# V of two chunks loaded behind the key transpose, and the crossbar transposes of those chunks issued in thirds, in a fused attention and feed-forward kernel

## The chip, the cores and the metric

The kernel runs on one core of one Trainium2 chip. The metric is device time in microseconds (us) of one execution. Before the change it is 226.85 us, the median of 3 runs.

## The reference

Attention with two kinds of heads feeds a feed-forward block with a leaky ReLU.

```python
# q, k, v: (4 batches, 8 heads, 768 positions, 64); is_retrieval = [1,0,1,0,0,0,1,0]; n_sink 4, window 64
scores = (1.0 / np.sqrt(D)) * np.matmul(q, k.transpose(0, 1, 3, 2))
# heads 0, 2, 6 ("retrieval"): causal.  The others ("stream"): causal, and only the
# first 4 keys (the sink) and the last 64 keys up to the query
a = softmax(np.where(mask, scores, -1e9))
attn = np.matmul(a, v)
x = attn.transpose(0, 2, 1, 3).reshape(B * S, H * D)      # 3072 x 512
h = x @ w_in                                              # 512 x 2048
out = np.maximum(0.01 * h, h) @ w_out                     # 2048 x 512, float32
```

All inputs and the output are float32 in HBM. The kernel computes in bfloat16 with float32 accumulation.

## The kernel before, in words

The 3072 rows are cut into 8 chunks of 384 positions: 4 batches times 2 halves. Chunks are worked in the order (batch 0, half 0), (1, 0), (0, 1), (1, 1), (2, 0), (3, 0), (2, 1), (3, 1), numbered 0 to 7; the change concerns chunks 2 and 3, the second halves of batches 0 and 1. Within a chunk, the three tiles of 128 positions are the "thirds".

Every chunk goes through four stages. Loads: `load_qk` (L113) and `load_v` (L121) issue, on GpSimd's queue, three DMAs each for K, Q and V, one for each third; such a DMA also converts float32 to bfloat16. Transposes: attention wants the head dimension on the partitions. For chunks 2 to 7 `turn_dma` (L240) does that with two crossbar DMA transposes on SyncE's queue, kb to kd for keys and qb to qd for queries, 128 x 1536 elements each. VectorE then copies the transposed keys into `kt` (`spreads`, L247, copies at L253: six for each chunk, one for each third and half of the heads). Stream heads read V shifted by 64 positions as well: `v_shift` (L147) writes `vb` from `va` by two DMAs on SyncE's queue (L151, L152), which wait for V to land. Attention: `Attention` (L294) issues scores (L345, L380) on TensorE, exponentials on ScalarE, masks on VectorE, and the products with V (L314), which read `va` and `vb`, some slots later. Feed-forward: `in_slots` multiplies by w_in (L585), and `Pair` (L720) multiplies by w_out (L753) with a seven-product scheme whose sums of weights and activations (L714, L736) and corrections (L768) VectorE makes.

The order on every engine is written out by hand: the tile framework runs in manual schedule mode, so instructions stand on an engine's queue in the order of the program, and waits are semaphores. The part around the change, with its lines:

- L886 to L890: the last loads issued ahead of the compute: three quarters of w_out, K and Q of chunk 2 (L888), the last quarter of w_out, V of chunk 2 (L890).
- L1008 to L1011: transposes of chunk 2, the shift of its V, then the loads of K, Q and V of chunk 3.
- L1018 to L1020: transposes of chunk 3, then the loads of K, Q and V of chunk 4. The shift of V of chunk 3 comes at L1032.
- L1034 to L1037: attention of chunk 2 merged with the feed-forward products of chunks 0 and 1; then the key copies of chunk 3.

The buffers kb and qb have one slot each, so loading the K of one chunk waits until the transpose of the chunk before has read it.[...] For two later chunks the kernel already holds GpSimd's queue back by a 1x1 copy into a tile `hold` that reads a tile written by a transpose (L1085).

Of the kernel before, what the change touches and what calls it, by code (L numbers as in the profile page):

```python
# [21 lines left out]
def kernel(  # L22
# [12 lines left out]
    nc = tc.nc  # L35
# [26 lines left out]
    def bf(name, *shape):  # L62
        return one.tile([128, *shape], BF16, name=name)
# [17 lines left out]
    hold = bf("hold", 1)  # L81
# [17 lines left out]
    raw = {}  # L99
# [13 lines left out]
    def load_qk(n, nms="kq"):  # L113
        b, c = ORDER[n]
        for nm in nms:
            t = rot.tile([128, 3, H, D], BF16, name=f"{nm}b", tag=f"{nm}b", bufs=1)
            raw[nm, n] = t
            for g in range(3):
                nc.gpsimd.dma_start(out=t[:, g], in_=nat[nm][b, c, :, :, g])  # L119

    def load_v(n, gs=range(3)):  # L121
        b, c = ORDER[n]
        for g in gs:
            nc.gpsimd.dma_start(out=va[b][:, 3 * c + g, :, 0:D], in_=nat["v"][b, c, :, :, g])  # L124

# [17 lines left out]
    def load_out(i):  # L143
        c = slice(4 * i, 4 * i + 4)
        nc.gpsimd.dma_start(out=w_out_bf[:, c, :], in_=w_out_r[:, c, :])

    def v_shift(n, eng=None):  # L147
        eng = eng or nc.sync
        i, c = ORDER[n]
        lo, hi = (0, 2) if c == 0 else (2, 5)  # L150
        eng.dma_start(out=vb[i][0:64, lo:hi], in_=va[i][64:128, lo:hi, 1:H])  # L151
        eng.dma_start(out=vb[i][64:128, lo:hi], in_=va[i][0:64, lo + 1 : hi + 1, 1:H])  # L152
# [87 lines left out]
    def turn_dma(n):  # L240
        qx[n] = rot.tile([128, 3, 4, 128], BF16, name="qd", tag="qd", bufs=3)
        raw["kx", n] = rot.tile([128, 3, 4, 128], BF16, name="kd", tag="kd", bufs=2)
        for nm, dst in (("k", raw["kx", n]), ("q", qx[n])):
            nc.sync.dma_start_transpose(out=dst.rearrange("p g q t -> p (g q) t"),
                                        in_=raw[nm, n].rearrange("p g h d -> p (g h d)"))

    def spreads(n):  # L247
        b, c = ORDER[n]
# [362 lines left out]
    for i, t in ((1, va[1]), (3, vb[1])):  # L611
        t = t.rearrange("p g h d -> p (g h d)")[:, 0 : 2 * KH * 512].rearrange("p (x g c) -> p x g c", x=2, g=KH)
# [98 lines left out]
    def weight_sums(half):  # L711

        r = slice(NH // 2 * half, NH // 2 * half + NH // 2)
        sub = lambda o, x, y: nc.vector.tensor_tensor(o[:, r], x[:, r], y[:, r], op=ALU.subtract)  # L714
        sub(w1, T3, B11)
        sub(w2, B22, w1)
        sub(T3, B22, T3)
        sub(w4, B21, w2)
# [76 lines left out]
    def tiles_of(n):  # L795
        return [tt for tt in range(3) if tt != spare(n)]
# [5 lines left out]
    for n in range(NCH):  # L802
        t = tiles_of(n)
# [66 lines left out]
    nc.gpsimd.iota(diff[:], pattern=[[1, 128]], base=0, channel_multiplier=-1, allow_small_or_imprecise_dtypes=True)  # L870
    load_tile(1)
    load_v(0, (0,))
    load_sinks(0)
    load_sinks(1)
    load_v(0, (1,))
    load_tile(2)
    load_v(0, (2,))
    load_in(0, 512)
    load_qk(1, "k")
# [7 lines left out]
        load_out(i)  # L887
    load_qk(2)  # L888
    load_out(3)
    load_v(2)  # L890


    nc.vector.tensor_scalar(ident[:], diff[:], 0.0, None, op0=ALU.is_equal)
# [13 lines left out]
    for a in (ats4[0], ats[0]):  # L907
# [4 lines left out]
                         in_=blank[:, 0:128].rearrange("p (o f) -> p o f", o=1).to_broadcast([128, 4, 128]), func=ACTF.Copy)  # L912
    nc.scalar.activation(out=ats[1][:, :, 1:3, :].rearrange("p j e f -> p j (e f)"),
                         in_=blank[:, 0:128].rearrange("p (o f) -> p o f", o=1).to_broadcast([128, 3, 128]), func=ACTF.Copy)
# [91 lines left out]
    zero_keys(1, nc.vector, CH, S)  # L1006
    nc.vector.memset(va[2][:, :, :, D], 1.0)
    turn_dma(2)  # L1008
    v_shift(2)
    load_qk(3)  # L1010
    load_v(3)  # L1011
    weight_sums(0)
    for i in range(1, 5):
        pairs[0].sum(i)
# [1 line left out]
    run(p1[:14], steps(0, ("P1",)), p1[14:])  # L1016
    weight_sums(1)
    turn_dma(3)  # L1018
    load_qk(4)
    load_v(4)  # L1020
    run(steps(1, ("P1",)), steps(0, ("P6", "P2")))
# [17 lines left out]
    for n in range(2, NCH):  # L1039
        a, extra = [], ()  # L1040
        if n + 2 < NCH:
            turn_dma(n + 2)
            v_shift(n + 2)
            extra = spreads(n + 2)
            if ORDER[n + 2][1] == 0:
                load_sinks(ORDER[n + 2][0])
            if n + 3 < NCH:
                load_qk(n + 3, "k" if n > 2 else "kq")
                if n < 3:
                    load_v(n + 3)  # L1050
            if ORDER[n + 2][1] == 0:
                sink_values(ORDER[n + 2][0], nc.gpsimd)
# [73 lines left out]
```

## Time and profile before

| what | value |
|---|---|
| median of 3 runs (lowest to highest) | 226.85 us (226.79 to 227.56) |
| profiled execution | 227.62 us, span 225.8 us, granted clock 1.00 |
| TensorE, VectorE, ScalarE, GpSimd busy | 95%, 66%, 60%, 32% of the span |
| DMA queue of GpSimd (software) | 77552 packets, 13.37 MB |
| DMA queue of SyncE (hardware) | 34336 packets, 15.14 MB |
| V third, issue to landing (24 of them) | least 2.7, median 7.0, most 14.3 us |
| crossbar transpose of a chunk's keys, issue to landing (6) | least 5.1, median 6.9, most 9.5 us, where the trace has it |

The span is the time from the first to the last instruction in one profiled execution. A timeline row gives the start, the duration, the engine, the line, the operation and its operands, and in brackets how long the engine stood idle before it and what ended that. Matmuls overlap in the pipeline: a row's duration includes its tail, and the distance between starts is the pace.

### The profile page before, as it was taken

To read this page: it belongs to the slowest core of one execution; us is meant where nothing else is said; L and a number is where in the kernel's file an instruction comes from. 1 tells how busy PE (TensorE), PEld (TensorE's weight loads), DVE (VectorE), ACT (ScalarE), POOL (GpSimd) and SP (SyncE) were. 2 spreads that over 40 slices of the span, in tenths; PEclk is the share of its full clock that TensorE was granted. 3 is DMA by queue.
4 is the path that set the end of the run, shared out by engine and by line. 5 is a ranking of instruction groups with operands and counts; after the bars stand their busy time and mean duration, and the time that the engine had idled before them with its cause. 6 is when DMAs were issued, how large, how long until landed. Compare 5 with 4: busy or idle time off the path is not lost.

```text
span 225.8 us, 5970 instructions
## 1 busy us (share of the span) xinstructions
PE 215.1 (95%) x2400; PEld 166.7 (74%) x2400; DVE 150.2 (66%) x408; ACT 136.1 (60%) x304; POOL 71.8 (32%) x88
## 2 busy tenths in 40 slices
PE   7898999998999999999999999999999999999993
PEld 4577766677887676786687777777787888788892
DVE  6684958968497656974477954354475867757662
ACT  4766865741884998367646553888456774446110
POOL 8968733405805806902449004400000000000000
PEclk9999999999999999999999999999999999999999
DMA  9999999999999999999969993998220130200232
GB/s 128 156 177 168 197 207 178 179 130 119 151 117 255 193 139 185 133 202 176 144 155 138 158 209 32 190 119 132 55 93 4 50 98 17 96 0 3 94 116 73
DMA packets 112972, 29.16 MB, mean 129 GB/s; under 512 B 102960, under 2 KB 110000, under 8 KB 112944
## 3 DMA queue, kind: packets, MB, share of 16 engines
q0 software_dynamic: 77552, 13.37, 82.7%
q1 hardware_dynamic: 34336, 15.14, 36.3%
q8 instruction: 19, 0.31, 0.6%
q10 hardware_dynamic: 1056, 0.26, 0.6%
q14 instruction: 9, 0.07, 0.1%
HBM read 27.30 MB, written 6.29 MB: 149 GB/s over the span
## 4 chain that ended last, share of the span: by engine, by line
PE 72%; DMA 16%; POOL 4%; DVE 4%; ACT 1%; issue 1%; POOLq 0%
PE ph L585 27%; PE py L753 20%; DMA qd<-qb 9%; DMA w_in_bf<-in_moe_w_in_dram 8%; PE po L314 6%; PE psS L345 5%; PE po L753 2%; PE psS L380 2%; PE ph L667 2%; PE psS L753 2%; PE psS L585 2%; POOL va L124 1%; POOL kb L119 1%; DVE sum L736 1%; PE po L667 1%; PE psS L667 1%
## 5 line engine op out<-in xcount | busy, mean ns | idle before, releaser
L585 PE MATMUL ph<-xt,w_in_bf 128*128 128x384 bf16 x384 | 75.1, 326 | 0.5 <-DMA w_in_bf<-in_moe_w_in_dram 0.5
L588 ACT ACTIVATE g_all<-ph 128x384 bf16<-128x384 f32 x96 | 47.1, 490 | 32.0 <-PE ph L585 30.7
L585 PEld LDWEIGHTS <-w_in_bf 128*128 128x128 bf16 x416 | 37.5, 97 | 18.9 <-DMA w_in_bf<-in_moe_w_in_dram 0.6
L350 ACT ACTIVATE at<-psS 128x384 bf16<-128x384 f32 x78 | 37.0, 489 | 15.3 <-PE psS L345 14.2
L753 PEld LDWEIGHTS <-sum 128*128 128x128 bf16 x408 | 36.7, 98 | 6.1 <-issue 1.2
L119 POOL DMA_DIRECT2D kb<-in_k_dram x21 | 18.9, 920 | 38.5 <-DMA kd<-kb 37.9
L753 PEld LDWEIGHTS <-g_all 128*128 128x128 bf16 x288 | 27.1, 98 | 5.1 <-issue 0.8
L753 PE MATMUL py<-w_sum,sum 128*128 128x256 bf16 (+1 forms) x184 | 25.6, 270 | 0.0
L345 PE MATMUL psS<-qd,kt 128*128 128x384 bf16 (+2 forms) x90 | 23.1, 294 | 1.1 <-DMA qd<-qb 1.1
L753 PE MATMUL py<-w_out_bf,sum 128*128 128x256 bf16 (+1 forms) x176 | 24.0, 270 | 0.1
L124 POOL DMA_DIRECT2D va<-in_v_dram x24 | 21.2, 904 | 2.3 <-DMA w_out_bf<-in_moe_w_out_dram 1.8
L119 POOL DMA_DIRECT2D qb<-in_q_dram x21 | 18.7, 909 | 6.2 <-DMA w_in_bf<-in_moe_w_in_dram 2.7
L736 DVE TENSOR_TENSOR sum<-g_all 128x1024 bf16<-128x1024 bf16 x25 | 17.5, 700 | 2.7 <-ACT g_all L588 2.4
L314 PE MATMUL po<-va,at 128*128 128x65 bf16 x228 | 19.3, 194 | 0.0
L389 DVE TENSOR_TENSOR ats<-ats,m_win 128x384 bf16<-128x384 bf16 x35 | 12.2, 356 | 10.2 <-ACT ats L385 9.6
L753 PE MATMUL py<-w_out_bf,g_all 128*128 128x256 bf16 x128 | 18.2, 272 | 0.4 <-DVE o L768 0.2
L385 ACT ACTIVATE ats<-psS 128x384 bf16<-128x384 f32 x35 | 16.7, 489 | 2.1 <-PE psS L380 1.9
L314 PEld LDWEIGHTS <-at 128*128 128x128 bf16 x234 | 14.4, 98 | 4.1 <-issue 0.5
L253 DVE COPY kt<-kd 64x512 bf16<-64x512 bf16 x36 | 12.7, 354 | 6.0 <-DMA kd<-kb 5.6
L413 DVE TENSOR_TENSOR xs<-po,linv 128x384 bf16<-128x384 f32 x27 | 15.1, 558 | 0.9
L768 DVE TENSOR_TENSOR u<-py,p 128x256 f32<-128x256 f32 x20 | 8.4, 422 | 8.2 <-PE py L753 7.6
L314 PEld LDWEIGHTS <-ats 128*128 128x128 bf16 x210 | 10.1, 97 | 3.1 <-DVE ats L389 0.5
(219 smaller groups left out, 340.7 us busy)
## 6 DMA issues: line engine op xcount, KB each, us to landing
out_dram<-o SPq DMA_DIRECT2D x23, 256.0 KB, 3.2
va<-in_v_dram POOLq DMA_DIRECT2D x24, 128.0 KB, 7.2
kb<-in_k_dram POOLq DMA_DIRECT2D x21, 128.0 KB, 5.9
qb<-in_q_dram POOLq DMA_DIRECT2D x21, 128.0 KB, 6.5
w_out_bf<-in_moe_w_out_dram POOLq DMA_DIRECT2D x4, 512.0 KB, 12.9
w_in_bf<-in_moe_w_in_dram POOLq DMA_DIRECT2D x3, 512.0 KB, 8.8
vb<-va SPq DMA_DIRECT2D x8, 170.6 KB, 5.0
w_in_bf<-in_moe_w_in_dram POOLq DMA_DIRECT2D x2, 256.0 KB, 8.3
```

The costliest lines, as they stand in the source:

```text
L119: nc.gpsimd.dma_start(out=t[:, g], in_=nat[nm][b, c, :, :, g])
L124: nc.gpsimd.dma_start(out=va[b][:, 3 * c + g, :, 0:D], in_=nat["v"][b, c, :, :, g])
L253: nc.vector.tensor_copy(kt[b % 2][hh][r, :, o : o + 128], raw["kx", n][r, g])
L314: nc.tensor.matmul(o, lhsT=lhsT, rhs=rhs, start=first, stop=False, skip_group_check=True)
L345: nc.tensor.matmul(s[:, off : off + w], lhsT=kt[i][hh][:, p, 128 * kj : 128 * kj + 128], rhs=q_of(n, p, lo, CH), start=(j == 0), stop=(j = ...
L350: nc.scalar.activation(out=a[:, 0:off], in_=s[:, 0:off], func=ACTF.Exp, scale=SM)
L385: nc.scalar.activation(out=av_, in_=s[:, 0:CH].rearrange("p (j e f) -> p j e f", j=3, e=2), func=ACTF.Exp, scale=SM)
L413: nc.vector.tensor_tensor(xs[:], po[:, :, :, 0:D], linv.to_broadcast([128, 3, 2, D]), op=ALU.mult)
L585: nc.tensor.matmul(ph[:, 0:CH], lhsT=w_in_bf[:, g, 128 * t : 128 * t + 128], rhs=xts[n][:, g, :] if n else xts[0][:, :, g, :], start=(g == ...
L588: nc.scalar.activation(out=g_all[:, slab(n) : slab(n) + 3, t, :], in_=ph[:, 0:CH].rearrange("p (j t) -> p j t", j=3), func=ACTF.Prelu, alp ...
L736: nc.vector.tensor_tensor(self.s[i], x, y, op=op)
L753: nc.tensor.matmul(s[:, 0 : c1 - c0], lhsT=lhs[:, j, :], rhs=rhs[:, j, c0:c1], start=first and j == 0, stop=(j == NH - 1), skip_group_chec ...
```

## The change

V of chunk 2 is no longer issued ahead of the compute. It is issued after `turn_dma(2)`, behind a 1x1 copy on GpSimd that reads the last third of the transposed keys, and ahead of the loads of K and Q of chunk 3. V of chunk 3 likewise moves from just behind the loads of K and Q of chunk 3 to behind `turn_dma(3)`, ahead of the loads of chunk 4. In `turn_dma`, for chunks 2 and 3, each of the two transposes is issued as three, one for each third, so that each waits only for the load of its own third; the later chunks keep one transpose each for keys and queries. On TensorE, VectorE and ScalarE the instructions and their order stay the same; only what they wait for differs.

```diff
-    def load_v(n, gs=range(3)):
+    def load_v(n, gs=range(3), behind=None):
         b, c = ORDER[n]
+        if behind is not None:
+            nc.gpsimd.tensor_copy(hold[0:1, :], behind)
         for g in gs:
             nc.gpsimd.dma_start(out=va[b][:, 3 * c + g, :, 0:D], in_=nat["v"][b, c, :, :, g])
...
         for nm, dst in (("k", raw["kx", n]), ("q", qx[n])):
-            nc.sync.dma_start_transpose(out=dst.rearrange("p g q t -> p (g q) t"),
-                                        in_=raw[nm, n].rearrange("p g h d -> p (g h d)"))
+            for g in [slice(j, j + 1) for j in range(3)] if n < 4 else [slice(0, 3)]:
+                nc.sync.dma_start_transpose(out=dst[:, g].rearrange("p g q t -> p (g q) t"),
+                                            in_=raw[nm, n][:, g].rearrange("p g h d -> p (g h d)"))
...
     load_qk(2)
     load_out(3)
-    load_v(2)
...
     turn_dma(2)
+    load_v(2, behind=raw["kx", 2][0:1, 2, 0, 0:1])
     v_shift(2)
     load_qk(3)
-    load_v(3)
...
     turn_dma(3)
+    load_v(3, behind=raw["kx", 3][0:1, 2, 0, 0:1])
     load_qk(4)
     load_v(4)
```

## The prediction

> **What bounds the kernel now.** I read busy shares and slices first, then the chain of waits in order of time, then the timelines of TensorE, GpSimd, SyncE and VectorE where that chain leaves TensorE. Page, parts 1 and 2:
>
> ```profile
> PE 215.1 (95%) x2400; PEld 166.7 (74%) x2400; DVE 150.2 (66%) x408; ACT 136.1 (60%) x304; POOL 71.8 (32%) x88
> ...
> PE   7898999998999999999999999999999999999993
> ...
> DMA  9999999999999999999969993998220130200232
> ```
>
> TensorE is busy 95% of the span at full clock, so a change to the loads can only win back TensorE's waits. The DMA row is nearly full for 27 of 40 slices, to about 150 us[...]. The chain of waits, 24 to 112 us (start, us, what):
>
> ```profile
> 44.24 11.46 DMA qd<-qb
> ...
> 55.75 0.50 PE psS L345 x2
> ...
> 64.16 8.14 DMA qd<-qb
> ...
> 72.33 0.32 PE psS L345
> ```
>
> After the start, and apart from pieces of 1 us and less, the chain leaves TensorE twice, each time for a crossbar transpose of queries: chunk 2's and chunk 3's. What those waits cost stands in TensorE's timeline:
>
> ```profile
> 54.12 1.04 PE L753 MATMUL po<-w_out_bf,g_all 128*128 128x256 bf16 x8
> 55.75 0.50 PE L345 MATMUL psS<-qd,kt 128*128 128x384 bf16 x2 [0.59 <-DMA qd<-qb]
> ...
> 71.49 0.33 PE L423 MATMUL ph<-ident,xs 128*128 128x128 bf16 x3
> 72.33 0.32 PE L345 MATMUL psS<-qd,kt 128*128 128x384 bf16 x1 [0.51 <-DMA qd<-qb]
> ```
>
> A busy time includes the pipeline's tail, so I use the pace. Eight 128x256 matmuls follow each other in 0.87 us (the rows from 53.25 to 54.12), so the first group is over at 54.99 and the next starts 0.76 late. Three 128x128 take 0.17, so the second wait is 72.33 - 71.66 = 0.67. Together 1.43 us, 0.63% of the time: all that the waits named in the chain can give.
>
> GpSimd's and SyncE's timelines show why the queries were late:
>
> ```profile
> 36.63 0.75 POOL L145 DMA_DIRECT2D w_out_bf<-in_moe_w_out_dram  x1 [1.28 <-DMA w_out_bf<-in_moe_w_out_dram]
> 39.16 2.79 POOL L124 DMA_DIRECT2D va<-in_v_dram  x3 [1.77 <-DMA w_out_bf<-in_moe_w_out_dram]
> 52.72 2.72 POOL L119 DMA_DIRECT2D kb<-in_k_dram  x3 [10.76 <-DMA kd<-kb]
> ```
>
> ```profile
> 41.91 2.15 SPq L244 DMA_TRANSPOSE kd<-kb  x1
> 44.24 5.77 SPq L244 DMA_TRANSPOSE qd<-qb  x1
> 52.45 0.71 SPq L151 DMA_DIRECT2D vb<-va  x1
> 55.39 0.62 SPq L152 DMA_DIRECT2D vb<-va  x1
> ```
>
> V of chunk 2 is issued from 39.16, just ahead of the transposes. Its thirds landed 10.8, 12.3 and 14.3 us after issue (50.0, 52.4, 55.4); the key transpose released GpSimd at 52.7, 10.8 after its issue, where the trace's median for such transposes is 6.9 and its least 5.1. From 52 to 54 us the queues moved 95 GB/s against 205 from 42 to 44: both kinds are slow while mixed.
>
> [...]a V third takes 2.7 us at best and 14.3 here.[...] So a wait put on GpSimd holds every load behind it; the trace shows such a wait, 10.76 us before the row at 52.72.[...] key copies L253 take 0.29 us in quiet and up to 0.70 beside GpSimd's issues.
>
> **The change, part by part.** *V moved behind the key transpose.* GpSimd gets one 1x1 copy per chunk, which waits for the transpose of the last third of keys; then three V issues. A copy of this kind took 0.28 (L1085), 0.5 from its start to the next issue. Behind it stand V and the loads of the next chunk. Call the landing of the last key third T.
>
> *Transposes in thirds.* SyncE issues six instead of two per chunk. The nearest row is xt's transpose (3 blocks against 4 here): 1.18 to 1.27 us to issue, so 6 x 1.2 = 7.2 us against 2.15 + 5.77 = 7.9: no loss, and V's shift, next on the queue, cannot go before V lands anyway. The first third may start at 39.9 (keys issued from 25.25, their first third landing 14.6 later), 2 us sooner than now; the last keys land at 41.8 (27.1 + 14.7), the last queries at 44.0.
>
> *T for chunk 2.* Early bound: last issue 42.3 plus xt's median of 4.1, 46.4. Late bound: as now, 52.7. The last piece of w_out still moves until 47.9 (36.63 + 11.3)[...]; a transpose with little beside it lands in 5.1. I take 49.5, and about 51 for the queries. TensorE wants those at 54.99: **first wait gone, -0.75**. With the early bound the gain is the same; with the late one the queries come as late as now and nothing is gained.
>
> *V then becomes the late one.* The shifted V needs T + 0.5 (copy) + 1.8 (two issues of 0.9 ahead) + 5.0 (key thirds issued from 52.72 landed in 4.4 to 5.7) + 4.5 (the shift of L152; L151 took 3.9, the median of such is 5.0) = T + 11.8 = 61.3. Its first reader stands at 62.17 and moves up to 61.4. That is no margin: half a microsecond more in any term is paid in full, since TensorE runs in order. I book **+0.3**; from the two ends of T, 0 to 3.1. Unshifted V (third 1 at T + 4.9) is wanted only at about 57.9 and is safe.
>
> *w_out beside earlier transposes.* VectorE takes up w_out at 48.02, TensorE needs the result at 49.3, VectorE is done at 48.6: 0.7 us of cover, so 0; up to +1 if transposes slow it by more.
>
> *Chunk 3.* Keys are issued at about 52.7 as now, queries 0.9 sooner, and V no longer runs into the transposes. T is then about 63.5 (now 69.8), queries about 65.5 against 71: the second wait goes. But VectorE's copies of the same keys come next:
>
> ```profile
> 72.63 2.59 DVE L253 COPY kt<-kd 64x512 bf16<-64x512 bf16 x6
> ```
>
> They stand behind a sum (72.03) on VectorE, itself behind a TensorE product, not behind the transpose. The fifth ends at 74.9, and the second 128x256 score of the TensorE row at 74.79 reads it. A TensorE 0.67 earlier meets it there: **-0.1**. Only if the copies ran at 0.29 each (fifth at 74.15) would all 0.67 come. GpSimd's issues after T (V, keys, queries and V of the next chunk, 4 x 2.65 us) last until 74.6 and go on disturbing them. Shifted V of chunk 3 is there at 63.5 + 11.8 = 75.3, wanted at 76.9: covered by 1.6 us.
>
> *Later loads.* All come some 5 us sooner. At 92.26 a sum on VectorE took 1.09 instead of 0.68 beside GpSimd's issue of V, and TensorE stood 0.3 at 93.74 behind it; likely gone: **-0.2** (0 to -0.3). After 100 us the chain is TensorE alone: 0.
>
> Sum: -0.75 + 0.3 - 0.1 - 0.2 = -0.75. The profiled execution took 227.62 us for a span of 225.8, so it would take 226.9; it lies 0.77 above the median of 226.85, from which I get **226.1 us**.
>
> **Rivals.** *Both waits go and the copies run undisturbed* (T early): -0.75 - 0.67 - 0.3 = -1.7, 225.1 us. For it: 61.5 to 70 us, where GpSimd is idle now, could hold the issues. Against it: the row at 74.79. *V too late*: the wait moves from the queries to the shifted V. Above T = 49.6 each microsecond is lost; at 50.3 the gain of chunk 2 is used up, from 51.5 the kernel is over 1.1 us slower. At T = 52: 61.4 becomes 63.8, net 2.4 - 0.75 = +1.65, 228.5 us; chunk 3 may add its part if its T passes 65. For it: transposes took 9.5 and 10.8 us here. Against it: those ran amid the V that is now taken away. *Nothing moves* (w_out, not V, slows the transposes): 226.9 us.
>
> **Chances.** Likeliest case 0.50, its own range 225.4 to 226.7; both waits gone 0.18; V too late 0.26; nothing 0.06. A difference of 0.5% (1.1 us) is about what a measurement of this kernel tells from none. Three tenths of the likeliest case lie beyond it: faster 0.15 + 0.18 = 0.33; same 0.35 + 0.06 = 0.41; slower 0.26. Range 224.9 to 228.6.
>
> **What would show it.** Right: no wait on qd at 55 or 72; T near 49.5 in GpSimd's timeline (its first V issue at 50); TensorE meeting a copied key near 74. Wrong: V issued after 51.5 and TensorE waiting for vb near 62 (or 77); VectorE waiting for w_out past 48.7; or copies of 0.29 throughout and a time under 225.4.

## The result, and the profile after

The changed kernel takes 234.33 us (median of 6 runs, 232.64 to 235.67) against 226.82 us (6 runs, 225.91 to 227.89): ratio 1.033 [1.029, 1.037]. It is 7.5 us slower, and the prediction of 226.1 us (range to 228.6) was wrong. The ratios here and below leave out executions that took over 1.5% more than the fastest of their kernel, so they need not equal the quotient of the medians. The profiled execution took 234.17 us, with a span of 232.2.

From the page after, parts 1 and 2:

```profile
PE 216.4 (93%) x2400; PEld 167.9 (72%) x2400; DVE 149.7 (64%) x408; ACT 135.7 (58%) x304; POOL 72.5 (31%) x90
...
PE   7898899999998269999999999999999999999994
...
PEclk9999999999999859999999999999999999999999
DMA  9999999999999999999929999799630022200222
```

TensorE's row has a hole of two slices (the 2 and the 6, about 75 to 87 us) that was not there before; the clock row has an 8 and a 5 beside it. The chain of waits, in order of time (start, us, what), says what fills the hole:

```profile
57.45 1.41 SPq L247
58.95 6.77 DMA kd<-kb
66.31 0.86 POOL va L126
68.03 6.35 DMA va<-in_v_dram
74.40 8.55 DMA vb<-va
83.08 0.49 PE po L317 x6
```

This is the new order itself, in chunk 3: key transpose, then V's issues, then V, then V's shift, then the first TensorE product that reads the shifted V. Nothing else stands between them. (Line numbers are 2 or 3 higher than before: the two shifts of V, L151 and L152, are now L153 and L154.)

TensorE's timeline, at the places that the prediction spoke of:

```profile
53.42 1.04 PE L756 MATMUL po<-w_out_bf,g_all 128*128 128x256 bf16 x8
54.30 0.49 PE L348 MATMUL psS<-qd,kt 128*128 128x384 bf16 x2
...
61.50 0.19 PE L317 MATMUL po<-vb,ats 128*128 128x65 bf16 x1 [0.51 <-DMA vb<-va]
...
71.33 0.32 PE L348 MATMUL psS<-qd,kt 128*128 128x384 bf16 x1 [0.69 <-DMA qd<-qb]
...
76.34 0.33 PE L348 MATMUL psS<-qd,kt 128*128 128x384 bf16 x1
83.08 0.22 PE L317 MATMUL po<-vb,ats 128*128 128x65 bf16 x1 [6.42 <-DMA vb<-va]
...
83.87 1.47 PE L588 MATMUL ph<-xt,w_in_bf 128*128 128x384 bf16 x4
...
87.57 0.81 PE L588 MATMUL ph<-xt,w_in_bf 128*128 128x384 bf16 x4
```

The first query wait is gone: eight products started at 53.42, and the scores follow at the pace of 0.87, at 54.30. There is a small wait for the shifted V of chunk 2 at 61.50, the second query wait is still there at 71.33, and at 83.08 comes the large one, for the shifted V of chunk 3. The last two rows are groups of four matmuls of one shape: 1.47 us at 83.87 and 0.81 at 87.57. TensorE's work behind the wait ran at half speed at first, as the windows' clock column (the number after the brackets of POOL, ahead of the DMA share) shows:

```profile
78.00:80.00 2.00, 0.00 (x0) 0.00 (x0) 0.00 (x0) 0.00 (x0) 0.00 (x0) 0.96 1.92 149
80.00:82.00 2.00, 0.00 (x0) 0.00 (x0) 0.00 (x0) 0.00 (x0) 0.00 (x0) 0.50 1.72 180
82.00:84.00 2.00, 0.92 (x11) 0.78 (x12) 0.00 (x0) 0.07 (x1) 0.00 (x0) 0.50 1.75 238
84.00:86.00 2.00, 2.00 (x13) 1.10 (x11) 0.75 (x2) 1.04 (x3) 0.00 (x0) 0.50 1.61 155
86.00:88.00 2.00, 2.00 (x30) 1.43 (x28) 0.52 (x2) 1.43 (x5) 0.00 (x0) 0.83 1.54 155
```

**Where the time went.** TensorE executes the same matmuls in the same order in both kernels, so I subtract the start of each matmul in the trace before from its start in the trace after. At 44 us (times of before) the changed run is 0.70 ahead; that comes from short waits before 30 us, most of them for loads, which differ between executions: in the traces of the experiments the same point lies between 1.28 ahead and 0.76 behind. From there:

| step | TensorE's lag changes by |
|---|---|
| first query wait gone (55) | -0.75 |
| up to the shifted V of chunk 2 | +0.11 |
| wait for the shifted V of chunk 2 (62.5) | +0.67 |
| short waits of before between 62.5 and 70 that take up part of it | -0.52 |
| second query wait (72.4), 0.86 instead of 0.67 | +0.18 |
| up to 76 | -0.11 |
| wait for the shifted V of chunk 3 (77.5) | +6.58 |
| half-speed stretch behind it (to 80) | +1.71 |
| from 80 to the end | -0.04 |

The sum is +7.83, all of it before 80 us on the scale of before. With the 0.70 of the start, the last matmul comes 7.13 later. The span is 6.4 longer; the remaining 0.7 lies behind the last matmul and was not followed. The half-speed part is that of one execution: the six of the changed kernel were granted between 0.976 and 0.993 of the full clock, the profiled one 0.985.

The queues after, GpSimd's and SyncE's timelines:

```profile
47.78 0.66 POOL L124 COPY hold<-kd 1x1 bf16<-1x1 bf16 x1 [11.09 <-DMA kd<-kb]
48.38 2.63 POOL L126 DMA_DIRECT2D va<-in_v_dram  x3
...
65.84 0.18 POOL L124 COPY hold<-kd 1x1 bf16<-1x1 bf16 x1 [9.36 <-DMA kd<-kb]
66.31 2.62 POOL L126 DMA_DIRECT2D va<-in_v_dram  x3 [0.29 <-issue]
68.90 2.65 POOL L119 DMA_DIRECT2D kb<-in_k_dram  x3
71.75 2.67 POOL L119 DMA_DIRECT2D qb<-in_q_dram  x3 [0.20 <-issue]
74.41 1.76 POOL L126 DMA_DIRECT2D va<-in_v_dram  x2
```

```profile
54.58 0.62 SPq L154 DMA_DIRECT2D vb<-va  x1
55.50 4.67 SPq L247 DMA_TRANSPOSE kd<-kb  x3
63.13 4.73 SPq L247 DMA_TRANSPOSE qd<-qb  x3
...
74.40 0.60 SPq L154 DMA_DIRECT2D vb<-va  x1
```

The two rows of `hold` give the landing of the last key third: 47.8 for chunk 2, 65.8 for chunk 3. The shift of chunk 3's V is issued at 74.40. By then six loads of chunk 4 have been issued, from 68.90 on, and the last three follow at the same moment. For comparison, rows of GpSimd, SyncE and TensorE before: the second such shift was issued at 69.56, 0.8 us ahead of chunk 4's first load, and its first reader did not wait. The two shifts whose landing that trace has, the first of chunk 2 and this one, took 3.9 and 5.0 us.

```profile
70.35 2.63 POOL L119 DMA_DIRECT2D kb<-in_k_dram  x3 [8.88 <-DMA kd<-kb]
69.56 0.59 SPq L152 DMA_DIRECT2D vb<-va  x1
77.62 0.19 PE L314 MATMUL po<-vb,ats 128*128 128x65 bf16 x1
```

### The profile page after: what moved, and what is told of

Same layout as the page of the kernel before. It is cut to its first block, busy times and chain, and to the rows that moved or that the text cites. A ratio compares the mean times of both kernels' runs of the same rounds, so it can differ in the third digit from the quotient of the medians.

```text
span 232.2 us, 5992 instructions
## 1 busy us (share of the span) xinstructions
PE 216.4 (93%) x2400; PEld 167.9 (72%) x2400; DVE 149.7 (64%) x408; ACT 135.7 (58%) x304; POOL 72.5 (31%) x90
## 4 chain that ended last, share of the span: by engine, by line
PE 69%; DMA 16%; POOL 5%; DVE 5%; issue 2%; ACT 1%; SPq 1%; POOLq 0%; ACTq 0%
PE ph L588 26%; PE py L756 20%; PE po L317 6%; PE psS L348 4%; DMA vb<-va 4%; DMA w_in_bf<-in_moe_w_in_dram 4%; DMA kb<-in_k_dram 3%; DMA kd<-kb 3%; DMA va<-in_v_dram 3%; PE po L756 3%; POOL va L126 2%; PE psS L588 2%; PE ph L670 2%; PE psS L383 2%; PE psS L756 2%
## 5 line engine op out<-in xcount | busy, mean ns | idle before, releaser
L588 PE MATMUL ph<-xt,w_in_bf 128*128 128x384 bf16 x384 | 76.1, 329 | 0.5 <-DMA w_in_bf<-in_moe_w_in_dram 0.5
L348 PE MATMUL psS<-qd,kt 128*128 128x384 bf16 (+2 forms) x90 | 23.7, 301 | 0.8 <-DMA qd<-qb 0.7
L392 DVE TENSOR_TENSOR ats<-ats,m_win 128x384 bf16<-128x384 bf16 x35 | 12.9, 373 | 12.6 <-ACT ats L388 12.2
L317 PE MATMUL po<-vb,ats 128*128 128x65 bf16 x88 | 10.0, 195 | 7.0 <-DMA vb<-va 6.9
L414 DVE RECIPROCAL linv<-po 128x6 f32<-128x6 f32 x27 | 5.2, 192 | 15.1 <-PE po L317 15.0
## 6 DMA issues: line engine op xcount, KB each, us to landing
vb<-va SPq DMA_DIRECT2D x8, 170.6 KB, 7.9
```

What stands on the lines that cost most here:

```text
L317: nc.tensor.matmul(o, lhsT=lhsT, rhs=rhs, start=first, stop=False, skip_group_check=True)
L348: nc.tensor.matmul(s[:, off : off + w], lhsT=kt[i][hh][:, p, 128 * kj : 128 * kj + 128], rhs=q_of(n, p, lo, CH), start=(j == 0), stop=(j = ...
L392: nc.vector.tensor_mul(av_, av_, m_)
L588: nc.tensor.matmul(ph[:, 0:CH], lhsT=w_in_bf[:, g, 128 * t : 128 * t + 128], rhs=xts[n][:, g, :] if n else xts[0][:, :, g, :], start=(g == ...
```

## The experiments

**Theory A**: the loss is V of chunk 3. Behind its key transpose V comes too late, and its shift runs beside chunk 4's loads. **Theory B**: the transposes in thirds are what delays chunk 3. **A third possibility**: the delay starts in chunk 2 and is carried on by SyncE's queue. The first four kernels take the parts of the change apart; the next three test what makes the shift slow; the last three look for what can be kept. All ratios are to the kernel before, run on the same chip.

### Thirds alone (e1_thirds_only)

```diff
     load_out(3)
+    load_v(2)
...
-    load_v(2, behind=raw["kx", 2][0:1, 2, 0, 0:1])
...
     load_qk(3)
+    load_v(3)
...
-    load_v(3, behind=raw["kx", 3][0:1, 2, 0, 0:1])
```

(against the changed kernel: both V back in their old places)

> The crossbar transposes of chunks 2 and 3 in thirds as in the changed kernel; V of both chunks loaded where it was before. Theory A (the loss of 7.5 us is V of chunk 3, moved behind its key transpose, whose shift then runs beside the loads of chunk 4): no wait of TensorE for vb over 0.3 us, time 225.5 to 228, the first shift of chunk 3 lands in under 6 us. Theory B (the thirds themselves stretch the transposes of chunk 3 in the midst of its loads, and everything behind comes late): 229 us or more, with the keys of chunk 3 transposed later than the 69.8 us of before. Whatever holds, the query wait near 55 us tells if the thirds alone win anything: 0 to -0.7.

Measured: 229.86 us, ratio 1.0128 [1.0094, 1.0163]. No wait for V, but the first query wait has grown, in TensorE's timeline:

```profile
57.24 0.49 PE L348 MATMUL psS<-qd,kt 128*128 128x384 bf16 x2 [2.40 <-DMA qd<-qb]
```

The scores start 2.57 us late instead of 0.76, and a half-speed stretch from 58.7 to 62.1 us follows:

```profile
58.00:60.00 2.00, 2.00 (x18) 1.42 (x16) 0.58 (x2) 1.64 (x5) 2.00 (x3) 0.67 1.86 150
60.00:62.00 2.00, 2.00 (x15) 1.34 (x14) 0.37 (x2) 1.16 (x3) 2.00 (x4) 0.50 2.77 144
62.00:64.00 2.00, 2.00 (x30) 1.60 (x29) 0.00 (x0) 1.47 (x5) 0.91 (x2) 0.97 4.57 118
```

That stretch is not in each of the 13 executions: seven were granted 0.999 of the full clock or more, the profiled one 0.993. So thirds by themselves, beside V, do harm, of another kind and size than the 7.5 us: theory A missed the time, which is in theory B's range, and was right that no wait for V is left.

### V alone (e2_v_only)

```diff
-            for g in [slice(j, j + 1) for j in range(3)] if n < 4 else [slice(0, 3)]:
+            for g in [slice(0, 3)]:
```

> V of chunks 2 and 3 moved as in the changed kernel; transposes whole as before. Theory A: V of chunk 3 still stands behind the keys' transpose and ahead of the loads of chunk 4, so TensorE waits 4 to 8 us for vb near 80 us and the time is 230 to 235. Theory B: without the thirds the transposes are quick, V of chunk 3 is issued before 63 us, the wait is under 1 us and the time 225.5 to 227.5.

Measured: 232.79 us, ratio 1.026 [1.019, 1.033]. GpSimd's copy behind the last key third of chunk 3, and two rows of TensorE:

```profile
64.80 0.49 POOL L124 COPY hold<-kd 1x1 bf16<-1x1 bf16 x1 [7.42 <-DMA kd<-kb]
...
75.11 0.23 PE L348 MATMUL psS<-qd,kt 128*128 128x128 bf16 x1 [0.45 <-DVE kt L256]
...
80.72 0.19 PE L317 MATMUL po<-vb,ats 128*128 128x65 bf16 x1 [2.77 <-DMA vb<-va]
```

Both query waits are gone (lag -0.75 at 55, -0.67 at 72.4). The second gain is given back, 0.16 where TensorE waits for ScalarE and 0.57 where it meets the key copies (the second row). The shifted V of chunk 3 then costs 2.9 (theory A expected 4 to 8), and the half-speed stretch 1.6 more. By the medians 6.1 of the 7.5 us need no thirds: theory B falls as the main cause.

The two traces give the thirds a larger share: from 44 us on TensorE's lag grows by 3.9 here and by 7.8 in the changed kernel. The thirds make the last key third of chunk 3 land later. The copy behind it starts at 64.80 here, in a run that was 1.46 us behind the changed one at 44 us, and at 65.84 there. With each run's lead or lag at 44 us taken off, that is 2.5 us later with thirds, and 1.8 to 2.2 later in the four other traces that have thirds and V of chunk 3 moved. So the two parts of the change add up in this wait, and how they share it is known only roughly.

### V of chunk 2 alone, or V of chunk 3 alone, with thirds (e3_v2_moved, e4_v3_moved)

```diff
# e3_v2_moved: V of chunk 3 back where it was
     load_qk(3)
+    load_v(3)
...
-    load_v(3, behind=raw["kx", 3][0:1, 2, 0, 0:1])
# e4_v3_moved: V of chunk 2 back where it was
     load_out(3)
+    load_v(2)
...
-    load_v(2, behind=raw["kx", 2][0:1, 2, 0, 0:1])
```

> The changed kernel, but V of chunk 3 is loaded where it was before (behind the queries of chunk 3); V of chunk 2 stays behind its key transpose, thirds in both chunks. Theory A: the wait of 6.6 us goes, what is left is chunk 2's exchange (queries no longer awaited, shifted V awaited 0.7 us): 225.5 to 227.5. Theory B: the thirds of chunk 3 still run into its loads, 229 or more. A third possibility, that V of chunk 2 delays the keys of chunk 3 by holding SyncE's queue: keys of chunk 3 transposed after 70 us and a query wait of over 1 us near 71.

> The changed kernel, but V of chunk 2 is loaded where it was before (ahead of the compute); V of chunk 3 stays behind its key transpose, thirds in both chunks. Theory A: nearly all of the loss remains, 231 to 236 us, with one wait of TensorE for vb of 5 to 8 us. Theory B: 229 to 235 too, so this run only tells both from the third possibility, that the delay starts in chunk 2 (V of chunk 2 holding SyncE's queue): then 226 to 228.

Measured: e3_v2_moved 228.27 us, ratio 1.0073 [1.0046, 1.0100]; e4_v3_moved 234.39 us, ratio 1.036 [1.028, 1.045]. One row of TensorE's timeline from each:

```profile
72.35 0.32 PE L348 MATMUL psS<-qd,kt 128*128 128x384 bf16 x1 [2.45 <-DMA qd<-qb]
```

```profile
81.43 0.21 PE L317 MATMUL po<-vb,ats 128*128 128x65 bf16 x1 [4.19 <-DMA vb<-va]
```

With V of chunk 3 in its old place the wait at 83 is gone; a query wait of 2.62 us in chunk 3 is left, and the time lies 0.8 us above theory A's range. Such a wait was named as a sign of the third possibility, but whole transposes in chunk 3 take it away (e6_v2_thirds, below): it is thirds beside V, as in e1_thirds_only. With V of chunk 3 moved the whole loss is there, though V of chunk 2 is where it was before. The loss goes with V of chunk 3 and needs no move in chunk 2: theory A holds for it, and the third possibility falls.

### What makes the shift slow (e5_loads4_after_shift, e9_v4_after_shift, e10_qv4_after_shift)

```diff
     load_v(3, behind=raw["kx", 3][0:1, 2, 0, 0:1])
-    load_qk(4)
-    load_v(4)
...
     v_shift(3)
+    nc.gpsimd.tensor_copy(hold[0:1, :], vb[1][64:65, 4, 0, 0:1])
+    load_qk(4)
+    load_v(4)
```

(e5. In e9 `load_qk(4)` stays where it was and only `load_v(4)` is held; in e10 the keys of chunk 4 stay and queries and V are held.)

> The changed kernel, with the loads of chunk 4's keys, queries and V held on GpSimd until chunk 3's V has been shifted (a 1x1 copy that reads the shifted tile stands ahead of them). In the changed kernel that shift (L154) was issued at 74.40, amid chunk 4's loads, and landed 8.55 us later; TensorE stood 6.4 us at 83.08, with the half-speed stretch behind it. Theory A1 (chunk 4's loads, issued right behind V, stretch V and its shift): V lands 4 to 5 us after its issue instead of 6.35, the shift takes 4 to 5 us instead of 8.55, the wait for the shifted V falls below 2 us and TensorE's clock stays near full there; behind it chunk 4's loads come 8 to 10 us later and may cost 0 to 2 us at chunk 4: 227 to 230 us. Rival A2 (a shift takes 7 to 8 us so soon after its load, whatever else moves): the wait stays at 4 to 6 us, 232 to 236 us. Rival A3 (the transposes of queries, not chunk 4's loads, slow V): V still takes over 6 us, the shift about 5, the wait 3 us, 230 to 232 us.

> The changed kernel with V of chunk 4 alone held on GpSimd until chunk 3's V has been shifted; keys and queries of chunk 4 follow chunk 3's V at once, as in the changed kernel. There the shift of chunk 3's V (L154) took 8.55 us, with all nine loads of chunk 4 held back 3.3 us. Theory D (dose: what moves beside the shift sets its time; six of nine loads are left): 6 to 7.5 us for the shift, a wait of 4 to 6 us for the shifted V, then a stretch at half clock, no wait for chunk 4's queries at 93: 231 to 233 us. Rival (V of chunk 4, issued from 74.41, just as the shift was, is what it queues behind): the shift falls to 4 to 5 us, the wait to 2 to 3 us, 228 to 230 us, and the kernel keeps most of what holding all of chunk 4 gained.

> The changed kernel with queries and V of chunk 4 held on GpSimd until chunk 3's V has been shifted; the keys of chunk 4 follow chunk 3's V at once. Theory D (dose; three of nine loads are left, issued 6 us ahead of the shift): the shift takes 4 to 5 us, the wait for the shifted V is 0 to 1.5 us at 77 to 80, and the queries of chunk 4, 8 us later than in the changed kernel, keep TensorE waiting 3 to 6 us near 92 (6.7 us with the keys held too): 230 to 233 us. Rival (chunk 4's keys alone, right behind V, stretch V's own landing): V takes over 6 us and the shift 6 to 7, the wait stays at 4 us, and with chunk 4's late queries behind it the time is 236 us or more.

Measured: 234.21 us, ratio 1.031 [1.026, 1.037] (e5); 232.06 us, 1.025 [1.019, 1.032] (e9); 230.37 us, 1.017 [1.011, 1.024] (e10). The view of the tile `vb`, from 50 to 84 us, ends with the time from issue to landing of the one shift it could follow, chunk 3's last; e9, e10 and e5 in this order:

```profile
DMA to landing us min/median/max: 7.3/7.3/7.3
```

```profile
DMA to landing us min/median/max: 3.4/3.4/3.4
```

```profile
DMA to landing us min/median/max: 3.1/3.1/3.1
```

| loads of chunk 4 not held (of 9) | shift of chunk 3's V | wait for it on TensorE | V's thirds issued to shift issued |
|---|---|---|---|
| 9 (after) | 8.55 us | 6.6 us | 66.3 to 74.4 |
| 9 (e4_v3_moved) | 8.2 us | 4.35 us | 65.4 to 73.1 |
| 9 (e2_v_only, whole transposes) | 7.6 us | 2.9 us | 65.3 to 73.0 |
| 6 (e9) | 7.3 us | 4.6 us | 66.1 to 74.0 |
| 3 (e10) | 3.4 us | 1.2 us | 66.1 to 74.8 |
| 0 (e5) | 3.1 us | 1.1 us | 65.2 to 72.9 |

The same DMA of the same size takes 3.1 or 8.55 us, according to what GpSimd issued ahead of it and at the same moment. The step is between three and six loads: the three key loads are issued by 71.4, three microseconds before the shift, and leave it alone; the three query loads (71.3 to 74.0 in e9) are the ones just ahead of it. Whether their number counts or their nearness was not separated.

Each line of the table is one trace. How far such traces scatter can be seen in chunk 2, where four of them (after, e5, e9, e10) have the same program up to the reader of the shifted V: it waited between 0 and 1.8 us. The step from three to six loads, 3.9 us, is wider than that; a difference between six and nine is not shown. The granted clock agrees with the step in every execution: the four of e9 had 0.985 to 0.993 of the full clock, the four of e10 0.998 or more.

Theory D, the dose, was right on both waits for V and on e9's shift; e10's shift came in under its 4 to 5 us, and chunk 4's queries cost less than its 3 to 6. In e10 what is held comes late in two places, 1.2 us for chunk 4's queries at 95 and 1.9 at 102, where a GpSimd operation behind the held loads is late. The rival of e5_loads4_after_shift, that a shift so soon after its load takes 7 to 8 us whatever moves, falls. V's own way does not get shorter: the last column spans 7.7 to 8.7 us in all six. V's last third takes 6.0 us in e5, with no load of chunk 4 issued, and 6.35 in the changed kernel. The third reading offered for e5_loads4_after_shift (V slow for another reason than chunk 4's loads) is thus right for V's landing, though not for the shift and the wait, and what makes V slow was not separated.

Why e5 is no faster than the changed kernel all the same (227 to 230 us were expected) stands in its VectorE timeline:

```profile
93.03 0.59 DVE L256 COPY kt<-kd 64x512 bf16<-64x512 bf16 x2 [10.13 <-DMA kd<-kb]
```

Chunk 4's keys, issued at 76.7 instead of 68.9, are transposed at 93.0, and TensorE stands still for 6.5 us there. The loads behind V cannot be late either: of the three orders tried, each loses at chunk 4 or at V, and e10 loses least.

### Chunk 2 alone (e8_v2_whole, e6_v2_thirds), and both V early (e7_v23_early)

```diff
# e8_v2_whole, against the changed kernel
-            for g in [slice(j, j + 1) for j in range(3)] if n < 4 else [slice(0, 3)]:
+            for g in [slice(0, 3)]:
...
     load_qk(3)
+    load_v(3)
...
-    load_v(3, behind=raw["kx", 3][0:1, 2, 0, 0:1])
# e6_v2_thirds: the same, but with "if n < 3" in the first line (thirds in chunk 2)
# e7_v23_early: as e8_v2_whole, but
     load_v(2, behind=raw["kx", 2][0:1, 2, 0, 0:1])
+    load_v(3)
     v_shift(2)
+    v_shift(3)
     load_qk(3)
```

> Only V of chunk 2 moved behind its key transpose; all transposes whole, chunk 3 as in the kernel before. With both V moved and whole transposes the first wait was gone (TensorE 0.75 us earlier at 55), no wait for the shifted V of chunk 2, and the loss came at chunk 3's shifted V. Theory: without the move in chunk 3 the gain of the first wait is left, and the second wait stays or grows a little since V of chunk 3 is no earlier than before: 225.5 to 227 us. Rival (any V load amid chunk 3's transposes now costs more because GpSimd is held at chunk 2): a second wait of over 2 us, 228 us or more.

> The change in chunk 2 alone: V of chunk 2 behind its key transpose, transposes in thirds in chunk 2 only; chunk 3 as in the kernel before. With V of chunk 3 in its old place and thirds in both chunks the time was 228.27 us, with a 2.62 us wait for chunk 3's queries at 72.35. Theory: thirds of chunk 3 beside V's software-queue load are what makes those queries late; with whole transposes there the wait falls back to 0.5 to 1 us, the first wait stays away, and the kernel comes to 225.5 to 227 us. Rival (V of chunk 3 coming later, since GpSimd is held in chunk 2, makes chunk 3's queries late by itself, whole or in thirds): the wait stays over 2 us, 228 us or more.

> V of chunks 2 and 3 both right behind chunk 2's key transpose, ahead of the keys and queries of chunk 3; all transposes whole; the shift of chunk 3's V right behind that of chunk 2's. Theory: V of chunk 3 is then out of the way of chunk 3's transposes and its shift is done ten microseconds before its reader; the second wait for queries goes if chunk 3's keys and queries, 2.7 us later in GpSimd's line, are not late by that themselves: 225 to 226.5 us. Rival (six V issues behind the key transpose make chunk 3's keys late, or the two V shifts on SyncE's queue hold chunk 3's transposes): a wait of 2 to 4 us for chunk 3's queries near 72, 228 to 231 us.

Measured: e8_v2_whole 226.70 us, ratio 0.9988 [0.9961, 1.0016]; e6_v2_thirds 226.82 us, 1.0023 [0.9990, 1.0055]; e7_v23_early 227.47 us, 1.0029 [1.0004, 1.0054]. In e8_v2_whole both query waits are gone in the trace and 0.19 of the second gain is left. Its lag goes from -0.57 at 44 us to -1.40 at the end, a gain of 0.83 us in that execution; over 22 runs it can't be told from no change. In e6_v2_thirds whole transposes in chunk 3 bring the query wait there down to 0.4, from 2.6 with thirds; the theory given with it holds, though not a gain in time. In e7_v23_early chunk 3's queries are late by 1.0 us; the likely reason is that their loads stand behind three more issues:

```profile
71.84 0.32 PE L348 MATMUL psS<-qd,kt 128*128 128x384 bf16 x1 [0.84 <-DMA qd<-qb]
```

No version was found that beats the kernel before by more than the measurement can tell.

## Why the prediction was wrong

**What bounds the kernel, and the first wait: right.** The key third of chunk 2 landed at 47.8 (taken: 49.5, an estimate between 46.4 and 52.7), the queries by 49.4, and -0.75 of lag is what was booked. That V beside them slows the transposes is shown by e1_thirds_only: with the same thirds and V in its old place, GpSimd was released at 54.1 instead of 47.8. The prediction's 95 against 205 GB/s does not show it, since V (39.2 to 55.4) and transposes (41.9 to 55.7) were in flight in both stretches.

**Shifted V of chunk 2: right within its range.** Booked +0.3 (0 to 3.1), measured +0.67. With T, the landing of the last key third, 1.7 us earlier than taken the sum would have cleared it; V landed in 4.4 us (taken: 5.0), but the shift took about 6.8 (taken: 4.5). The mis-sized term already shows here, hidden by an early T. That the result came close to the 0.3 is luck: over the four traces with the same program up to there (after, e5, e9, e10), TensorE's wait lay between 0 and 1.8 us. The step has no margin, as the prediction said.

**w_out, and SyncE's issues in thirds: booked at nothing.** VectorE waited 1.0 us for w_out at 46.5, and TensorE did not follow. SyncE issued chunk 2's six thirds in 8.7 us (estimated: 7.2; whole, before: 7.9). Missing was what thirds do to the landing: beside V's loads 2.57 us of query wait in e1_thirds_only and 2.62 in e3_v2_moved, and in the changed kernel a later T in chunk 3.

**Chunk 3: this step failed.** The prediction's sentence is "Shifted V of chunk 3 is there at 63.5 + 11.8 = 75.3, wanted at 76.9: covered by 1.6 us". By its own terms:

| term | taken | measured |
|---|---|---|
| T, last key third of chunk 3 | 63.5 | 65.8 |
| copy and two V issues | 2.3 | 2.2 |
| V, last third | 5.0 | 6.35 |
| shift of V | 4.5 | 8.55 |
| shifted V there | 75.3 | 82.95 |

Of the 7.65 us that it came late, 4.05 are the shift, 2.3 are T and 1.35 V. T is the term of the thirds: with whole transposes (e2_v_only) it came near what was taken, 64.0 (64.80 less the 0.76 by which that run was behind at 44 us). The shift is the largest term, and moving V is what mis-sized it. Its 4.5 was put between the two landings of the trace before, 3.9 and 5.0, for shifts ahead of which at most three loads of the next chunk had been issued; the change puts V and its shift behind T, and so six loads of chunk 4 get in front. The prediction saw those issues ("last until 74.6") and charged them to the key copies, not to the shift. That the shift's time depends on them is measured (3.1 us with none of them ahead of it, 8.55 in the changed kernel); why it does was not shown. The price of chunk 2 was carried over to chunk 3 as if the neighbours were the same. The rival "V too late" had the right mechanism and even a threshold for chunk 3 ("if its T passes 65"; it was 65.8), but chunk 3's part was left without a price.

**The half-speed stretch was not in the sum at all**: 1.71 us, a fifth of the loss. The trace before gives no price for it: its granted clock is 1.00, and the longest wait of its TensorE is 1.1 us. The clock column of the later traces gives the length: the half-speed time in the windows is 6.8 us in the changed kernel (0.16 + 6.0 + 0.68), in e4_v3_moved, e5_loads4_after_shift and e9_v4_after_shift, and 3.4 in e1_thirds_only and e2_v_only. With the stretch measured here, a rival with a wait of 4 us or more would carry 1.7 us on top.

**The key copies, -0.1 out of 0.67: right in kind.** In the profiled execution of the changed kernel the second query wait stayed, so the step was never reached there. Where the wait went and GpSimd was issuing, the copies took back 0.57 (e2_v_only), 0.33 (e8_v2_whole), 0.51 (e4_v3_moved) and 0.69 (e9_v4_after_shift), on either side of the 0.57 (0.67 less 0.1) that the prediction took off. The other half of that step holds too: in e5_loads4_after_shift and e10_qv4_after_shift, where GpSimd issues nothing at that time, six copies follow each other in 1.88 us instead of 2.39 to 2.77, and they take nothing back (e5: lag -1.87 before the wait, -2.44 at 75).

**The second query wait and the later loads: not as said.** Chunk 3's queries landed at 71.2, not 65.5: in thirds they came behind the keys, whose last third took 6.8 us. (Before they landed at 64.16 + 8.14 = 72.3, where the prediction reads 71.) But the wait of 0.86 us is that of one execution: in e9_v4_after_shift, whose program is the same up to there, and in e4, e5 and e10, the queries in thirds landed at 68.7 to 69.2 and the wait was gone, as with whole transposes in e2_v_only and e8_v2_whole. The -0.2 of the later loads was not seen in the changed kernel, whose lag is constant from 80 us on; in seven of the ten experiments TensorE gains 0.3 there.

Of the signs named as "wrong", TensorE waiting for the shifted V was the one that came, near 62, and near 77, where it then stood until 83; V of chunk 2 was not issued late (48.4).

## What to carry to other kernels

When a load is moved behind a wait, price it with the neighbours of its new place: list what its queue-mates issue between the wait's end and the landing, and take a duration from a row that ran beside as much. In a chain of dependent DMAs (load, then shift) price each link by itself: here the loads behind V hardly touched its landing (6.0 or 6.35 us) and stretched the shift from 3.1 to 8.55. A later stage can be more crowded than an earlier one (8.55 against about 6.8 us). Add the half-speed stretch to a long TensorE wait: in these traces each wait of 2.9 us or more had one, which cost 1.6 to 2.7 us.

## What the runs showed of the hardware

- The time of one shift of 170.6 KB depends sharply on the loads issued just ahead of it: 3.4 us with three of them, the last issued three microseconds before (e10_qv4_after_shift), and 7.3 us with six (e9_v4_after_shift).
- TensorE's clock was halved for 3.4 or 6.8 us, after waits of 2.57 (e1_thirds_only), 2.9 (e2_v_only) and 4.35 to 6.7 us, but not after one of 2.62 (e3_v2_moved). In e1_thirds_only the drop came 1.5 us after the work had resumed.
- The length of a wait alone does not decide whether the clock drops: it did around one of 2.57 us and not around one of 2.62, as above. In the changed kernel's trace the record of the granted clock has 75.09 us at full speed and then 6.83 at half; the 3.4 of e1_thirds_only and e2_v_only is half of that. Whether it also counts where a wait lies, and where the limit is, was not shown.
- Three transposes of a third each landed later than one of three thirds where V was loaded beside them, though the first of them could start earlier: query wait 2.57 against 0.76 us in chunk 2 (e1_thirds_only, before), 2.62 against 0.4 in chunk 3 (e3_v2_moved, e6_v2_thirds).
